# Linear attention and a highway layer on one core: one batch's query turned by DMA, weights in the output buffers, a new list of steps

## The chip, the core and the metric

The kernel runs on one core of a Trainium2 chip. The metric is the device time of one execution in microseconds (us). The engines work beside each other, each through its own list of instructions in order: PE (matrix products and transposes), DVE (vector operations), ACT (activations and copies, and some DMA issues), POOL (vector operations that do not touch PSUM), and SP, whose list holds DMA issues. An instruction waits at the head of its list until what it needs is there.

## The reference

With q, k and v of 8 batches, 8 heads, 576 positions and 64 columns each:

```
q_s = softmax of q over the 64 columns
k_s = softmax of k over the 576 positions
kv  = k_s^T v          # 64 x 64 for each batch and head
x   = q_s kv           # regrouped to 4608 tokens x 512
H   = max(x w_h, 0);  T = sigmoid(x w_t + b_t)
out = T * H + (1 - T) * x
```

Inputs and output are 32 bit floats; the kernel computes its products in 16 bit floats with sums in 32 bits.

## The kernel before

**Tiles.** A token p*9+j of a batch lies on partition p (64 of them) with j from 0 to 8, and two heads share the 128 partitions. A tile has 128 tokens: for each batch four tiles with two values of j, and for each pair of batches one tile with j = 8 of both. That makes 36 tiles; 0 to 3 belong to batch 0, 4 to 7 to batch 1, 8 to both, and so on; 27 to 30 belong to batch 6, 31 to 34 to batch 7, 35 (`LAST`) to both. `mate` names the neighbour with which a tile is stored.

**A batch.** `k`, `v`, `q` load it (three buffers of each). `ek` and `eq` are the exponentials on ACT, `vc` casts v. `kv` makes 72 small products (with a column of ones that gives the sum over positions), `kr` and `kn` divide by that sum and lay the result out in `kvb`. `qt` turns the exponentials of q in three groups (L280: eight, eight and two transposes of 128x128 on PE, into the PSUM tile qps), and `qc` (L291) copies each group out to the tile eq.

**A tile.** `xu` multiplies turned q by kv, with the sums of q beside; `rs` and `x` divide (DVE). `xt` turns x on PE, `xe` copies it out. `bw` seeds the PSUM bank of the gate with the bias: on ACT as a copy of a ready 128x512 tile, or on PE as one matmul. `mt` adds x w_t (four matmuls of 512 columns) and `mh` makes x w_h - x/2 with a weight that was halved and had half the identity subtracted (`whc`, `whd`). `th` is tanh of half the gate (ACT), `dd` the maximum of -x/2 and the product (DVE), `uu` is (tanh + 1) times d, and `oo` adds x (POOL). Where `uu` is marked `:P` the tile is "lifted": `ee` on POOL makes d + x, `uu` on POOL makes tanh times d, and `oo` adds these two; ACT's tanh then goes to SBUF. `st` stores.

**Order.** The order is written out by hand: `ORDER` (L16) is a list of steps, such as `xu_9_0` or `xe_9_0:D`, that the last loop (L433) works through; a suffix says which engine (A for ACT, D for DVE, P for POOL). Every engine gets its own instructions in this order. Nothing else places work; the tile framework adds the waits. `fill_n` is n matmuls on a blank tile, whose result nobody reads; they stand only ahead of the first large products. The loads are issued on SP, between the stores.

**Buffers.** Results of two mates share a 128x2x512 buffer of 32 bit floats (tag o32, three buffers); single tiles have 128x512 (tag o1). d, u, tanh and e of tiles have three buffers each (pool dp). PSUM has two banks for the gate (tps), two for the other product (gps), two for xu or kv, one for qps, one for the turned x.

**Steps that the prediction names.** `load_w` L191 and the weights' landing tiles L108; casts L199 to L211; `eq` L273; `qt` L280; `qc` L291; `xu` L299; `bw` L344; `mt` L354; `mh` L360; `th` L372; `ee` L385; `uu` L390; `oo` L403; `st` L414. The last tile's gate is worked in two halves of 256 columns, in one bank; its four stores of 64 rows and 256 columns go two on SP and two on ACT (L418).

Of the kernel before, what the change touches and what calls it, by code (L numbers as in the profile page):

```python
# [16 lines left out]
b_0 b_32 setuppool fill_16 setupdve k_0_0 v_0_0 v_0_2 k_0_2 q_0_0 w_h_0 q_0_4 bsplit w_h_2 fill_4 bp w_t_0 bc vc_0_0:A  # L17
w_t_2 bw_0:A ek_0_1 vc_0_2 k_1_0 ek_0_0 vc_0_3 vc_0_1:A ek_0_3 fill_30 kv_0_0 q_1_0 ek_0_2 kr_0_0 kn_0_0 fill_5 kv_0_1
eq_0_0 v_1_0 kr_0_1 kn_0_1 fill_6 qt_0_0 whc_0 k_1_2 qc_0_0 half fill_9 xu_1_0 xu_0_1 xu_0_0 eq_0_1 rs_0_1 rs_1_0
v_1_2 rs_0_0 x_1_0 bw_1:A x_0_0 fill_10 qt_0_1 x_0_1 whd_0 qc_0_1:A q_1_4 fill_2 xt_0_1 whc_2 xt_0_0 whd_1 whd_3  # L20
xe_0_1 fill_6 xu_2_0 whd_2 xe_0_0 xt_1_0 rs_2_0 mh_0_0 v_2_0 xe_1_0 x_2_0 mh_0_1 eq_0_2 wtc_0:D mh_1_0 wtc_2:D mt_0_0
dd_1 mt_0_1 dd_0 xu_3_0 th_0_0 xt_2_0 mt_1_0 rs_3_0 k_2_0 xe_2_0:D ek_1_0 uu_0_0 mh_2_0 th_1_0 x_3_0 eq_1_0 bw_2
uu_1_0 xt_3_0 mt_2_0 dd_2 ek_1_1 xe_3_0:D qt_1_0 oo_0_0 oo_1_0 q_2_0 th_2_0 vc_1_1:D mh_3_0 bw_3:A uu_2_0 ek_1_2
mt_3_0 qc_1_0 ek_1_3 dd_3 th_3_0 vc_1_0 oo_2_0 kv_1_0 vc_1_2 vc_1_3:A kr_1_0 st_1_0_0 uu_3_0 kv_1_1 kn_1_0 k_3_0 bw_4
kr_1_1 kn_1_1 eq_1_1 xu_5_0 eq_1_2 qt_1_1 rs_5_0 x_5_0 xu_4_0 bw_5 qc_1_1:A rs_4_0 st_1_0_1 xt_5_0 x_4_0 xu_4_1 v_3_0
qt_1_2 xu_6_0 vc_2_0:A qc_1_2:A q_3_0 xe_5_0:D rs_4_1 mh_5_0 x_4_1 rs_6_0 x_6_0 xt_4_0 mt_5_0 xe_4_0:D dd_5 xu_7_0
th_5_0 xt_4_1 mt_4_0 oo_3_0 rs_7_0 xe_4_1 mh_4_0 ek_2_2 xt_6_0 qt_0_2 mt_4_1 mh_4_1 ek_2_0 th_4_0 uu_5_0 xe_6_0:D
x_7_0 mh_6_0 dd_4 vc_2_2 oo_5_0 kv_2_0 uu_4_0 xt_7_0 kr_2_0 bw_6 bw_7:A qc_0_2:A eq_2_0 oo_4_0 dd_6 mt_6_0 kn_2_0
eq_2_1 qt_2_0 ee_6 st_5_0_1 xe_7_0:D xu_8_0 st_3_0_1 th_6_0 qc_2_0 mt_7_0 st_3_0_0 rs_8_0 uu_6_0:P bw_8:A k_4_0 x_8_0
qt_2_1 ek_3_2 xu_9_0 xt_8_0 mh_7_0 rs_9_0 x_9_0 xe_8_0 st_5_0_0 eq_2_2 xt_9_0 dd_7 ek_3_0 v_4_0 xu_10_0 mt_8_0 rs_10_0  # L30
oo_6_0 xe_9_0:D th_7_0 x_10_0 mh_8_0 th_8_0 uu_7_0 vc_3_0:A xt_10_0 mh_9_0 dd_8 xe_10_0:D vc_3_2 oo_7_0 q_4_0 bw_9:A
kv_3_0 uu_8_0 qc_2_1:A oo_8_0 bw_10 mh_10_0 kr_3_0 kn_3_0 eq_3_0 dd_9 xu_11_0 eq_3_1 mt_9_0 st_7_0_1 rs_11_0 ee_9
x_11_0 qt_3_0 st_7_0_0 th_9_0 dd_10 xt_11_0 xu_12_0 q_5_0 xe_11_0:D mt_10_0 uu_9_0:P rs_12_0 qc_3_0 mh_11_0 x_12_0
th_10_0 uu_10_0 xu_13_0 xt_12_0 ek_4_0 bw_11 rs_13_0 mt_11_0 xe_12_0:D x_13_0 k_5_0 eq_3_2 bw_12 dd_11 qt_2_2 th_11_0
xu_14_0 xt_13_0 ek_4_2 oo_9_0 oo_10_0 mt_12_0 rs_14_0 qc_2_2 uu_11_0 qt_3_1 x_14_0 xe_13_0 mh_12_0 bw_13:A qc_3_1
v_5_0 th_12_0 xt_14_0 xu_15_0 dd_12 xe_14_0 mh_13_0 rs_15_0 oo_11_0 vc_4_0:A uu_12_0 mh_14_0 x_15_0 bw_14 dd_14
st_10_0_0 eq_4_0 dd_13 st_10_0_1 vc_4_2 oo_12_0 kv_4_0 qt_3_2 mt_13_0 kr_4_0 qc_3_2 kn_4_0 k_6_0 xt_15_0 mt_14_0
th_13_0 xe_15_0 uu_13_0 xu_16_0 th_14_0 qt_4_0 rs_16_0 oo_13_0 mh_15_0 bw_15:A x_16_0 eq_4_1 uu_14_0 xu_17_0 qc_4_0
xt_16_0 oo_14_0 eq_5_0 bw_16 mt_15_0 xe_16_0:D rs_17_0 eq_5_2 x_17_0 mt_16_0 st_14_0_0 th_15_0 st_12_0_1 dd_15 xt_17_0
st_12_0_0 xu_18_0 th_16_0 uu_15_0:P xe_17_0:D mh_16_0 v_6_0 bw_17:A rs_18_0 x_18_0 ek_5_2 qt_4_1 ee_15 dd_16 xu_19_0  # L40
xt_18_0 ek_5_0 mh_17_0 rs_19_0 qc_4_1 xe_18_0:D qt_5_0 x_19_0 vc_5_0:A vc_5_2 q_6_0 mt_17_0 qc_5_0 xt_19_0 dd_17
kv_5_0 th_17_0 oo_15_0 uu_16_0 st_14_0_1 qt_5_2 mh_18_0 kr_5_0 bw_18:A xe_19_0:D kn_5_0 bw_19:A mt_18_0 dd_18 xu_20_0
mt_19_0 rs_20_0 x_20_0 qc_5_2:A eq_5_1 th_18_0 qt_5_1 ek_6_2 xu_21_0 xt_20_0 mh_19_0 xe_20_0 uu_18_0 rs_21_0 x_21_0
bw_20:A xt_21_0 dd_19 th_19_0 xu_22_0 mt_20_0 qc_5_1:A rs_22_0 oo_16_0 uu_17_0:P st_16_0_0 ee_17 oo_17_0 oo_18_0
uu_19_0 mh_20_0 x_22_0 xe_21_0 oo_19_0 th_20_0 xt_22_0 xu_23_0 dd_20 bw_21:A mh_21_0 vc_6_2 bw_22:A rs_23_0 x_23_0
eq_4_2 mt_21_0 uu_20_0:P ek_6_0 xe_22_0:D q_7_0 dd_21 qt_4_2 st_16_0_1 xu_24_0 mt_22_0 th_21_0 vc_6_0 k_7_0 rs_24_0
x_24_0 v_7_0 eq_6_0 mh_22_0 uu_21_0 ee_20 st_19_0_1 xt_23_0 th_22_0 qc_4_2 kv_6_0 st_19_0_0 xe_23_0:D bw_23:A oo_21_0
dd_22 eq_6_1 st_17_0_1 xt_24_0 qt_6_0 kr_6_0 kn_6_0 mh_23_0 xe_24_0 qc_6_0 eq_7_0 xu_25_0 mt_23_0 rs_25_0 x_25_0
bw_24:A qt_7_0 dd_23 eq_7_2 xu_26_0 th_23_0 xt_25_0 oo_20_0 uu_22_0:P st_21_0_0 ee_22 mh_24_0 rs_26_0 uu_23_0 oo_22_0
x_26_0 mt_24_0 xe_25_0:D dd_24 xu_27_0 xt_26_0 rs_27_0 oo_23_0 xe_26_0:D st_23_0_1 x_27_0 st_8_0_0 st_8_0_1 vc_7_2  # L50
st_21_0_1 qc_7_0:A bw_25:A ek_7_2 mt_25_0 th_24_0 qt_6_1 ek_7_0 uu_24_0 xt_27_0 xu_28_0 xe_27_0:D mh_25_0 th_25_0
rs_28_0 x_28_0 vc_7_0:A mh_26_0 dd_25 xt_28_0 bw_26:A kv_7_0 dd_26 eq_7_1 uu_25_0 mh_27_0 kr_7_0 qc_6_1:A kn_7_0
# [14 lines left out]
def kernel(  # L67
# [28 lines left out]
    op = pool("op", 3)  # L96
# [11 lines left out]
    w32 = {w: consts.tile([P, KC, DM], FP32, name="w32" + w) for w in "th"}  # L108
# [13 lines left out]
    def once(name, make):  # L122
        if name not in T:
            T[name] = make()
        return T[name]
# [15 lines left out]

    def columns(i, h):
        return slice(h * DM // 2, (h + 1) * DM // 2) if i == LAST else slice(0, DM)
# [47 lines left out]
    def load_w(e, w, c):  # L191
        src = dict(t=moe_w_t, h=moe_w_h)[w]
        nc.sync.dma_start(w32[w][:, c:c + 2], src.rearrange("(c p) n -> p c n", p=P)[:, c:c + 2])
# [5 lines left out]
    def wt_cast(e, c):  # L199
        if e == "D":  # L200
            nc.vector.tensor_scalar_mul(w16["t"][:, c:c + 2], w32["t"][:, c:c + 2], 1.0)
        else:
            nc.scalar.copy(w16["t"][:, c:c + 2], w32["t"][:, c:c + 2])

    def wh_cast(e, c):
        nc.vector.tensor_scalar_mul(w16["h"][:, c:c + 2], w32["h"][:, c:c + 2], 0.5)

    def wh_diag(e, c):
        cs = slice(c * P, (c + 1) * P)
        nc.vector.scalar_tensor_tensor(  # L210
            w16["h"][:, c, cs], w32["h"][:, c, cs], 0.5, half, op0=ALU.mult, op1=ALU.subtract)  # L211
# [60 lines left out]

    def eq(e, b, g):  # L273
        t = once(f"qe{b}", lambda: qep.tile([P, NJ, 4, D], FP16, tag="qe", name=f"qe_{b}"))
        j0, j1 = GROUPS[g]
        nc.scalar.activation(t[:, j0:j1].rearrange("p j c d -> p c j d"),  # L276
                             T[f"q32{b}"].rearrange("p c (j d) -> p c j d", j=NJ)[:, :, j0:j1], AF.Exp)
# [20 lines left out]

    def xu(e, i, k):  # L299
# [7 lines left out]
        for n in range(2 * k0, 2 * k1):  # L307
            kk, hh = n // 2, n % 2
            for w, b in enumerate(bs):
                rows = slice(0, P) if len(bs) == 1 else slice(64 * w, 64 * w + 64)  # L310
                dst = t[rows, kk - k0, 0:260].rearrange("p (s e) -> p s e", s=4)[:, hh:hh + 3:2]
                nc.tensor.matmul(dst, T[f"eq{b}_{jp // 2}"][:, jp % 2, n], kvb[b % NKV][:, hh, kk],  # L312
# [31 lines left out]
    def bw(e, i):  # L344
        t = T[f"tps{i}"] = ps_t.tile([P, DM], FP32, tag="tps", name=f"tps_{i}")
        if e == "A":
            nc.scalar.copy(t, ball)  # L347
        else:
            nc.tensor.matmul(t, ones, b16, start=True, stop=False, skip_group_check=True)
# [117 lines left out]
```

The softmax here doesn't subtract the row's maximum and nothing guards it: scores larger than these inputs give would overflow.

## Time and profile before

| what | value |
|---|---|
| three runs | 125.98, 126.94, 127.22 us |
| median | 126.94 us |
| span of the profiled execution, first to last instruction | 126.1 us |
| mean granted clock of PE | 0.977 |
| PE busy, instructions | 112.1 us, 1415 |
| DVE busy | 101.4 us, 237 |
| ACT busy | 92.8 us, 144 |
| POOL busy | 70.2 us, 71 |
| moved by DMA | 40.08 MB |
| matmul of 128x512, gate (L357) | 140 |
| transposes of q (L286) | 144 of 222 ns, eight in a row take 0.45 us |
| u on DVE, 128x512 (L396) | 27 of 687 ns |
| e, u on POOL (L388, L394) | 8 each, 1157 and 1155 ns |
| o on POOL (L412) | 27 of 1155 ns from u and x, 8 of 1154 ns from u and e |
| v cast of 128x1152 on POOL (L238) | 1143 ns |
| w_t cast of 128x1024 on DVE (L201) | 684 ns |
| copy of a turned group of q, 128x1024 (L295) | 677 ns on DVE, 1010 on ACT |

Times are us from the first instruction unless marked ns. A matmul's busy time is longer than the distance to the next, since matmuls are pipelined, so distances are taken from the starts in the timeline. "[1.19 <-DVE kvb L266]" at the end of a line of the timeline says how long the engine was idle ahead of it and what ended that. In the slices each digit is the busy share of a fortieth of the span in tenths. The rows of an engine ending in q (SPq, ACTq) are the issues of DMAs.

### The profile page before, as it was taken

The page shows a single profiled execution, that of the slowest core. Times are in us where ns is not written, and L with a number is a line of the kernel's source. Part 1 is how long each engine was busy: PE and PEld are TensorE (multiplying, and loading weights), DVE is VectorE, ACT ScalarE, POOL GpSimd, SP SyncE. Part 2 cuts the span into 40 slices and gives each one's busy share as a digit, 9 for nine tenths or more (in the row PEclk, how much of TensorE's full clock was granted, in tenths as well). Part 3 has the DMA queues.
Part 4 walks back from the last instruction along what each step waited for, and adds up shares of the span by engine and source line. Part 5 has one row for each costly group of instructions (what it writes and reads, how often), then busy time and mean ns, then how long its engine had stood idle before and what let it go on. Part 6 is the DMA issues. An engine that isn't in the chain of part 4 may idle for free.

```text
span 126.1 us, 3549 instructions
## 1 busy us (share of the span) xinstructions
PE 112.1 (89%) x1415; PEld 68.6 (54%) x1415; DVE 101.4 (80%) x237; ACT 92.8 (74%) x144; POOL 70.2 (56%) x71
## 2 busy tenths in 40 slices
PE   5798979994999799999999999999899999999800
PEld 4485854543755365556564666557456656555400
DVE  5504769996868779999989899989889989999640
ACT  4098363995747999968959979999899996557500
POOL 5030000485304694785716769999974896786610
PEclk9999999999599999999999999999999999999996
DMA  4999999999999999999999999999987363733994
GB/s 110 376 386 373 383 385 377 387 378 387 391 394 400 396 385 300 376 394 396 405 393 391 402 404 397 393 400 394 393 324 229 86 166 83 144 70 80 222 237 127
DMA packets 20372, 40.08 MB, mean 318 GB/s; under 512 B 1282, under 2 KB 3586, under 8 KB 20356
## 3 DMA queue, kind: packets, MB, share of 16 engines
q1 hardware_dynamic: 20192, 39.72, 90.1%
q8 instruction: 11, 0.18, 0.6%
q10 hardware_dynamic: 164, 0.14, 0.4%
q14 instruction: 5, 0.04, 0.1%
HBM read 30.41 MB, written 9.44 MB: 316 GB/s over the span
## 4 chain that ended last, share of the span: by engine, by line
PE 36%; DMA 22%; DVE 12%; POOL 9%; ACT 7%; SPq 5%; issue 3%; DVEq 0%; POOLq 0%; ACTq 0%
PE gps L363 11%; DMA q<-in_q_dram 9%; PE tps L357 9%; DMA w32h<-in_moe_w_h_dram 7%; POOL o L412 6%; DMA out_dram<-o 5%; PE xu L312 5%; PE qps L286 4%; DVE u L396 4%; PE turned L334 3%; DVE d L383 2%; ACT qe L276 2%; ACT ek L232 2%; PE kv L248 2%; PE turned L168 2%
## 5 line engine op out<-in xcount | busy, mean ns | idle before, releaser
L412 POOL TENSOR_TENSOR o<-u,x 128x512 f32<-128x512 f16 x27 | 31.2, 1155 | 33.2 <-DVE u L396 32.7
L363 PE MATMUL gps<-w16h,xT 128*128 128x512 f16 x144 | 36.9, 384 | 0.0
L357 PE MATMUL tps<-w16t,xT 128*128 128x512 f16 (+1 forms) x148 | 36.8, 373 | 0.0
L327 DVE TENSOR_TENSOR x<-xu,rs 128x512 f16<-128x512 f32 (+1 forms) x38 | 24.9, 659 | 1.2
L383 DVE SCALAR_TENSOR_TENSOR d<-x,gps 128x512 f16<-128x512 f16 x36 | 24.3, 679 | 1.0 <-PE gps L363 0.8
L379 ACT ACTIVATE tps<-tps 128x512 f32<-128x512 f32 (+1 forms) x29 | 16.4, 568 | 11.0 <-PE tps L357 9.6
L276 ACT ACTIVATE qe<-q 128x1024 f16<-128x1024 f32 (+1 forms) x24 | 19.8, 845 | 3.0 <-DMA q<-in_q_dram 3.0
L396 DVE SCALAR_TENSOR_TENSOR u<-tps,d 128x512 f16<-128x512 f32 (+1 forms) x29 | 19.3, 669 | 3.1 <-POOL o L412 1.4
L357 PEld LDWEIGHTS <-xT 128*128 128x128 f16 x148 | 13.6, 98 | 11.6
L363 PEld LDWEIGHTS <-xT 128*128 128x128 f16 x144 | 13.2, 99 | 11.9 <-issue 0.5
L232 ACT ACTIVATE ek<-k 128x1152 f16<-128x1152 f32 (+1 forms) x20 | 18.8, 966 | 0.2 <-DMA k<-in_k_dram 0.2
L347 ACT COPY tps<-ball 128x512 f32<-128x512 f32 x27 | 15.9, 594 | 3.4 <-DVE u L396 3.4
L238 POOL CAST v<-v 128x1152 f16<-128x1152 f32 (+1 forms) x11 | 10.6, 969 | 10.8 <-DMA v<-in_v_dram 9.6
L312 PE MATMUL xu<-kvb,eq 128*128 128x130 f16 (+1 forms) x160 | 15.0, 229 | 1.4 <-DVE kvb L266 1.2
L334 PE MATMUL turned<-idh,x 128*128 128x128 f16 x144 | 14.4, 222 | 0.2 <-ACT xT L341 0.2
L168 PE MATMUL turned<-blank 128*128 128x256 f16 x88 | 12.4, 295 | 2.2 <-POOL blank L147 1.3
L312 PEld LDWEIGHTS <-eq 128*128 128x128 f16 (+1 forms) x160 | 10.3, 103 | 6.1 <-DVE kvb L266 1.7
L286 PE MATMUL qps<-idh,qe 128*128 128x128 f16 x144 | 12.3, 222 | 1.3 <-ACT qe L276 1.2
L334 PEld LDWEIGHTS <-x 128*128 128x128 f16 x144 | 9.8, 99 | 6.0 <-DVE x L327 2.7
L286 PEld LDWEIGHTS <-qe 128*128 128x128 f16 x144 | 9.5, 99 | 5.5 <-ACT qe L276 2.5
L168 PEld LDWEIGHTS <-blank 128*128 128x128 f16 x88 | 9.0, 106 | 4.1 <-POOL blank L147 1.3
L394 POOL TENSOR_TENSOR u<-th,d 128x512 f16<-128x512 f16 x8 | 9.2, 1155 | 2.8 <-ACT th L377 1.3
(45 smaller groups left out, 111.4 us busy)
## 6 DMA issues: line engine op xcount, KB each, us to landing
out_dram<-o SPq DMA_DIRECT2D x28, 256.0 KB, 9.6
v<-in_v_dram SPq DMA_DIRECT2D x6, 1152.0 KB, 13.5
k<-in_k_dram SPq DMA_DIRECT2D x6, 1152.0 KB, 13.9
q<-in_q_dram SPq DMA_DIRECT2D x6, 1152.0 KB, 14.0
k<-in_k_dram SPq DMA_DIRECT2D x4, 576.0 KB, 9.4
v<-in_v_dram SPq DMA_DIRECT2D x4, 576.0 KB, 6.6
out_dram<-o SPq DMA_DIRECT2D x14, 128.0 KB, 3.0
q<-in_q_dram SPq DMA_DIRECT2D x2, 640.0 KB, 11.4
```

Source lines behind the costliest of these rows:

```text
L168: nc.tensor.matmul(spare, blank[:, 0:P], blank[:, 0:2 * P], start=True, stop=True, skip_group_check=True)
L232: nc.scalar.activation(t[:, :, c:c + n].rearrange("p j c d -> p c j d"), T[f"k32{b}"][:, c:c + n].rearrange("p c (j d) -> p c j d", j=NJ), ...
L276: nc.scalar.activation(t[:, j0:j1].rearrange("p j c d -> p c j d"), T[f"q32{b}"].rearrange("p c (j d) -> p c j d", j=NJ)[:, :, j0:j1], AF.Exp)
L286: nc.tensor.matmul(t[:, (j - j0) // 2, 2 * kk:2 * kk + 2, (j - j0) % 2], T[f"qe{b}"][:, j, 2 * kk:2 * kk + 2].rearrange("p c d -> p (c d)" ...
L312: nc.tensor.matmul(dst, T[f"eq{b}_{jp // 2}"][:, jp % 2, n], kvb[b % NKV][:, hh, kk], start=True, stop=True, skip_group_check=True)
L327: nc.vector.tensor_mul(t[:, k0:k1], sums(i, k)[:, :, :, 0:64], T[f"rs{i}_{k}"][:, 0:k1 - k0].unsqueeze(3).to_broadcast([P, k1 - k0, 4, D]))
L334: nc.tensor.matmul(t[:, n], T[f"x{i}"][:, n * P:(n + 1) * P], idh, is_transpose=True, start=True, stop=True, skip_group_check=True)
L357: nc.tensor.matmul(T[f"tps{i}"][:, cs], T[f"xT{i}"][:, n], w16["t"][:, n, cs], start=False, stop=(n == 3), skip_group_check=True)
L363: nc.tensor.matmul(t, T[f"xT{i}"][:, n], w16["h"][:, n], start=(n == 0), stop=(n == 3), skip_group_check=True)
L383: nc.vector.scalar_tensor_tensor(t, T[f"x{i}"], -0.5, T[f"gps{i}"], op0=ALU.mult, op1=ALU.max)
L396: nc.vector.scalar_tensor_tensor(t[:, cs], T[f"tps{i}"][:, cs], 1.0, T[f"d{i}"][:, cs], op0=ALU.add, op1=ALU.mult)
L412: eng.tensor_add(t[:, cs], T[f"u{i}"][:, cs], T[f"{'e' if lifted(i) else 'x'}{i}"][:, cs])
```

## The change

It has six parts.

1. **Batch 7's query is turned by DMA.** Steps `dt_7_0` and `dt_7_1` each issue one transposing DMA on SP from the exponentials (64 partitions of 18 x 128 halves of 16 bits each) into a new tile eqd. `eq` writes batch 7 in another layout, two activations of 128x1152 in place of three; `qt_7` and `qc_7` are gone, and `xu` takes its weights from eqd.
2. **Weights land in output buffers.** The pool of o32 has seven buffers in place of three; the four loads of 128x2x512 weights take four of them first, and the separate tiles of weights in 32 bits are gone. w_t can be cast on POOL, and is.
3. **The last tile.** Each half of its gate has its own PSUM bank (the second takes that of qps), seeded on its own; its o halves go to POOL and DVE; its halves are stored with one DMA each, both batches in one (tile 8, 17 and 26 too).
4. **Stores on either queue.** A store marked `:A` is issued by ACT: nine are, in place of two.
5. **Halved tiles.** Tiles 0 and 4 may take their halves in either order.
6. **A new list of steps.** Lifted tiles are 0, 1, 2, 3, 4, 7, 8, 10, 11, 12, 14, 16, 18, 20, 21, 25, 27, 28 (18 in place of 8); bias seeds on PE are those of 0, 1, 2, 3, 4, 5, 7 and half of 35 (in place of 2, 4, 5, 6, 10, 11, 12, 14, 16); fills are 122 in place of 88.

The diff, cut:

```
-b_0 b_32 setuppool fill_16 setupdve k_0_0 v_0_0 v_0_2 k_0_2 q_0_0 w_h_0 q_0_4 bsplit w_h_2 fill_4 bp w_t_0 bc vc_0_0:A
-w_t_2 bw_0:A ek_0_1 vc_0_2 k_1_0 ek_0_0 vc_0_3 vc_0_1:A ek_0_3 fill_30 kv_0_0 q_1_0 ek_0_2 kr_0_0 kn_0_0 fill_5 kv_0_1
-eq_0_0 v_1_0 kr_0_1 kn_0_1 fill_6 qt_0_0 whc_0 k_1_2 qc_0_0 half fill_9 xu_1_0 xu_0_1 xu_0_0 eq_0_1 rs_0_1 rs_1_0
...
+b_0 b_32 q_0_0 v_0_0 eq_0_0 setupdve k_0_0 bsplit k_0_2 v_0_2 setuppool ek_0_0 vc_0_0 fill_30 vc_0_3 fill_30 q_0_4 half
+qt_0_0 w_h_0 ek_0_3 vc_0_1:D w_h_2 bp fill_30 w_t_0 ek_0_2 qc_0_0:A vc_0_2:D bc ek_0_1 w_t_2 fill_12 kv_0_0 eq_0_1
+kr_0_0 kv_0_1 kn_0_0 bw_0 qt_0_1 bw_3 kr_0_1 kn_0_1 xu_0_0 k_1_0 v_1_0 xu_1_0 whc_0 qc_0_1:A xu_0_1 wtc_0:P wtc_2:P
+rs_1_0 rs_0_1 whc_2 rs_0_0 eq_0_2 vc_1_1 x_0_0 x_1_0 whd_2 fill_20 x_0_1 xu_3_0 v_1_2 xt_0_0 xt_0_1 k_1_2 xe_0_0 xe_0_1
+q_1_0 q_1_4 whd_0 rs_3_0 xt_1_0 mt_0_0 mt_0_1 whd_3 xe_1_0 x_3_0 whd_1 mh_0_1 ek_1_0 mh_1_0 xu_2_0 xt_3_0 qt_0_2 mh_0_0
...
+oo_19_0 ee_21 rs_26_0 th_23_0 xe_25_0:D st_7_0_0 uu_21_0:P bw_24:A mh_23_0 eq_7_1 x_26_0 mh_24_0 xt_26_0 dd_23 xu_27_0
+eq_7_0 v_7_0 uu_23_0 oo_21_0 bw_25:A rs_27_0 oo_22_0 mt_24_0 xe_26_0:D eq_6_2 st_10_0_1 x_27_0 mh_25_0 dd_24 xu_29_0
+dt_7_0 ek_7_2 st_8_0_0 dt_7_1 mt_25_0 xt_27_0 dd_25 rs_29_0 th_24_0 vc_7_2:A oo_23_0 mh_26_0 vc_7_0 x_29_0 xe_27_0:D
...
+th_35_1 st_33_0_1 uu_34_0 dd_35 uu_35_1 th_35_0 st_33_0_0:A uu_35_0 oo_34_0 st_34_0_0 oo_35_0 st_34_0_1:A oo_35_1:D
+st_35_1_0 st_35_0_0:A
...
-    op = pool("op", 3)
+    op = pool("op", 7)
...
-    w32 = {w: consts.tile([P, KC, DM], FP32, name="w32" + w) for w in "th"}
...
-        nc.sync.dma_start(w32[w][:, c:c + 2], src.rearrange("(c p) n -> p c n", p=P)[:, c:c + 2])
+        T[f"w{w}{c}"] = op.tile([P, 2, DM], FP32, tag="o32", name=f"w32{w}_{c}")
+        nc.sync.dma_start(T[f"w{w}{c}"], src.rearrange("(c p) n -> p c n", p=P)[:, c:c + 2])
...
+        if b in BY_DMA:
+            t = once(f"qe{b}", lambda: qep.tile([P, 2 * NJ, 2 * D], FP16, tag="qe", name=f"qe_{b}"))
+            nc.scalar.activation(
+                t[:, g * NJ:g * NJ + NJ].rearrange("p j (w d) -> p w j d", w=2),
+                T[f"q32{b}"][:, 2 * g:2 * g + 2].rearrange("p w (j d) -> p w j d", j=NJ), AF.Exp)
+            return
...
+    def dt(e, b, hh):
+        t = once(f"eqd{b}", lambda: eqp.tile([P, 2, 2 * NJ, NP], FP16, tag="eqd", bufs=2, name=f"eqd_{b}"))
+        eng = nc.scalar if e == "A" else nc.sync
+        eng.dma_start(t[:, hh], T[f"qe{b}"][NP * hh:NP * hh + NP], transpose=True)
+
+    def turned_q(b, jp, n):
+        if b not in BY_DMA:
+            return T[f"eq{b}_{jp // 2}"][:, jp % 2, n]
+        j = (n // 2) * NJ + 2 * jp
+        return T[f"eqd{b}"][:, n % 2, j:j + (2 if jp < 4 else 1)].rearrange("p s t -> p (s t)")
...
+    def bw(e, i, h=0):
+        bank = (ps_t, "tps") if i < LAST or h == 0 else (ps_q, "qps")
+        t = T[gate(i, h)] = bank[0].tile([P, DM], FP32, tag=bank[1], name=f"tps_{i}_{h}")
...
-        eng = nc.vector if e == "D" or i == LAST else nc.gpsimd
+        eng = nc.vector if e == "D" else nc.gpsimd
...
-        eng = nc.scalar if i == LAST and r else nc.sync
+        eng = nc.scalar if e == "A" else nc.sync
...
-            eng.dma_start(dst[:, 8], T[f"o{i}"][rows, cs])
+            ends = out[b * S:(b + 2) * S, cs].rearrange("(r j) n -> r j n", j=NJ)
+            eng.dma_start(ends[:, 8], T[f"o{i}"][:, cs])
```

SP's own order of loads and stores around the change: before, it is q_5, k_5, v_5, two stores of tile pair 10, k_6, three stores (14, 12, 12), v_6, q_6, two stores, q_7, one store, k_7, v_7. After, it is v_5, k_5, one store of pair 1, q_5, v_6, one store of pair 10, k_6, one store, q_6, three stores (7, 3, 5), q_7, k_7, one store, v_7, one store, dt_7_0, the store of 8, dt_7_1, and the rest of the stores; ACT issues two stores of pairs 3 and 1 shortly ahead of the seed of tile 16.

## The prediction

> **What bounds the kernel now.** I read the page's slices first, then the windows of 5 us, then the timeline around the weak windows and the end. The slices (each 3.15 us):
>
> ```profile
> PE   5798979994999799999999999999899999999800
> POOL 5030000485304694785716769999974896786610
> PEclk9999999999599999999999999999999999999996
> DMA  4999999999999999999999999999987363733994
> ```
>
> DMA is full until about 91 us, PE from about 45 us to its last matmul, POOL is half empty. DMA is not the end: the last batch's loads land at 89.6 (q, the chain of waits) and about 96 (v, awaited by POOL), and PE has work until 119.2. The weak windows (columns: window, its length, busy us of PE, PEld, DVE, ACT, POOL, granted clock, DMA share, GB/s):
>
> ```profile
> 20.00:25.00 5.00, 5.00 (x34) 2.51 (x33) 4.80 (x10) 3.16 (x7) 1.23 (x2) 1.00 1.07 389
> 25.00:30.00 5.00, 4.03 (x92) 2.29 (x90) 4.54 (x10) 4.93 (x9) 4.22 (x5) 1.00 1.05 378
> 30.00:35.00 5.00, 4.01 (x31) 2.84 (x32) 4.03 (x13) 2.55 (x4) 1.53 (x2) 0.66 1.05 389
> 40.00:45.00 5.00, 4.17 (x80) 2.58 (x69) 3.98 (x9) 4.30 (x7) 3.18 (x3) 1.00 1.05 396
> 105.00:110.00 5.00, 5.00 (x38) 2.85 (x37) 4.71 (x10) 2.81 (x6) 3.04 (x3) 1.00 0.61 127
> ```
>
> PE loses 1.0, 1.0 and 0.8 us in three of them, and from 30 to 35 the clock drops to 0.66. The timeline names the places:
>
> ```profile
> 19.30 1.89 PE L363 MATMUL gps<-w16h,xT 128*128 128x512 f16 x8
> ...
> 30.99 0.41 PE L312 MATMUL xu<-kvb,eq 128*128 128x130 f16 x4 [1.19 <-DVE kvb L266]
> ...
> 33.73 1.64 PE L363 MATMUL gps<-w16h,xT 128*128 128x512 f16 x4
> ...
> 42.57 0.62 PE L286 MATMUL qps<-idh,qe 128*128 128x128 f16 x8 [0.83 <-ACT qe L276]
> ...
> 118.18 1.04 PE L357 MATMUL tps<-w16t,xT 128*128 128x256 f16 x8
> ...
> 120.93 0.76 DVE L412 TENSOR_TENSOR o<-u,x 128x256 f32<-128x256 f16 x2
> 121.39 1.18 ACTq L425 DMA_DIRECT2D out_dram<-o  x2
> 122.36 1.20 SPq L425 DMA_DIRECT2D out_dram<-o  x2
> ```
>
> The large products start at 19.3; batch 1's first xu waits for its kv chain; four large matmuls at 33.7 take 1.64 instead of 1.03 (about 0.6 lost); PE ends at 119.2 and the span 6.9 us later, through tanh, u, o and four small stores. So the bound is PE's in-order list, with a slow opening and a serial tail.
>
> [...]
>
> **The change, part by part.** Large matmuls follow each other every 0.216 us in the timeline (four in 0.865), so a tile costs PE 1.73, plus xu 0.235 and its own transposes 0.22.
>
> *Batch 7's query off PE.* 18 of 144 transposes go. Eight take 0.45 in the chain of waits, so 18 x 0.056 = 1.0 us off PE. The three evictions (two of 128x1024, one of 128x256) go too; eq_7 becomes two activations of 128x1152 (1.16 by the ek row) for 1.06 + 1.06 + 0.42.
>
> *Fewer bias matmuls.* 9 become 7 and a half: 1.5 x 0.215 = 0.3 off PE; ACT gets one more seed of 0.594 and a half one (0.37, by the 128x256 tanh).
>
> *Who does what.* Lifted tiles (u and e on POOL) go from 8 to 18. DVE: 10 u x 0.687 = -6.9, two casts of w_t -1.3, the other moves nearly cancel (about +0.3): 101.4 to 93.5. POOL: 10 x (1.155 + 1.157) = +23.1, two v casts fewer -2.3, two w_t casts +2.0 (1.143 x 1024/1152 each), half an o +0.6: 70.2 to 93.6. ACT stays near 93, but issues 9 stores instead of 2 (0.54 each: +3.8 us of its queue). Two of them (tiles 3 and 1) stand before the seeds and tanh of tiles 14 to 16; their o are long done, so I charge the issue alone, hidden since ACT has 8 to 30% idle in the windows from 50 us on, save some full ones; without that cover tanh, then u, is late by the same 0.54 each.
>
> *Opening.* Bytes to each load at 379 GB/s with the observed landing of w_h_0 (3.4 MB, 12.8) give w_t_2 at about 18.6 in both. The new list puts 90 fills ahead of kv_0_0 plus 12: 20 cold at about 0.175, then 0.112 each, 3.5 + 9.2; with qt_0_0 and bp in between (0.9) and a start at 1.3, kv_0_0 comes at 14.9 (9.67 before). Then kr/kn to 17.05, the first xu, 20 fills to 19.75, x_0_1 at 20.8 behind whc and whd on DVE, xe, xt_1_0, and mt_0_0 at 21.7: 2.4 later than before's first product. I keep this loss. Against it: v_1_2 and k_1_2 are loaded ahead of q_1_0, kv_1_0 is fed earlier, and bw, xt_2 and the products of tile 2 stand where PE stood idle. Walking the PE list by these durations, with ek_1_3 at 28.7 and eq_1_0 at 29.8 on ACT, I get mh_5 ended at 35.9 with xu_6 and qt_0_2 already done, where before has the rest at 36.2: 0.3 + 0.24 + 0.11 = 0.65 ahead. Then kv_2 at 41.4, after more work than in before, and xu_9 behind mh_7, so that kn_2's latency is covered: tiles 0 to 7 and xu_9 are done at 44.6 and qt_2_2 too, against 46.14: 1.5 ahead.
>
> *Loads and stores.* 9 stores of 0.26 MB stand before v_7 instead of 16: 7 x 0.26 / 0.39 = 4.7 us earlier. Seven output buffers allow that (the weights' 16 KB a partition are reused). I cost it at nothing: PE from 45 to 119 has only some 2.2 us of idle, which this does not remove. If stores came first, q_7 would again be just in time (wait of 0.4 at qps).
>
> *Middle and end of PE.* From 44.6, 28 tiles x 1.73 = 48.4, 26 xu and the pairs 6.7, xt 5.95, four batches of qt 4.05, five kv 3.6, a half bias: 68.8; with the same 2.2 idle PE ends at 115.6. Before's own sum from 46.14 is 70.9 + 2.2 = 119.2. So PE ends 3.6 us earlier: 1.5 from the opening, 2.1 here (1.0 transposes, 0.1 the qt_2_2 already done, 1.0 for the five bias matmuls that before still has in this stretch).
>
> *Transposing DMAs.* eq_7_1 and eq_7_0 follow th_23: by the list after it mt_23 ends at 87.7, so eq_7_0 at about 91.2, when the loads (v_7 about 91) are in. The first use, xu_31, has 14 half products (12.1) and 2.3 of xu and xt after it: 115.6 - 14.4 = 101.2. Both together have 10 us. Each moves 64 x 1152 x 2 bytes = 147 KB. [...] The new wait is SP's, for eq_7_0: behind it stand st_8, st_14 and every later store of SP, and behind those POOL's o, when the seven buffers are full. In a 10 us hold POOL makes four o, two pairs, so this cover is thin if the stores have fallen behind; then o waits, u's buffers fill, and DVE is next.
>
> *Last tile.* Halves in their own banks, one store each, on SP and ACT, o halves on POOL and DVE at once. After PE's end: tanh 0.37, u 0.42, o on POOL 0.58 (half of 1.155), hops of 0.1, an issue of 0.6, landing 2.2, end 0.5: 5.2 instead of 6.9, -1.7.
>
> **Sum.** 126.1 - 3.6 - 1.7 = 120.8. POOL now has 62 us of work in the 70 us from 44 on and three buffers of d, and ACT issues stores amid its work: I add 0.8 for such waits, 121.6, 4.5 less. The profiled span of 126.1 is within the runs (125.98 to 127.22); from their median of 126.94 I forecast 122.4.
>
> **Rivals.** *A, POOL becomes the bound.* For: tiles 0, 1, 3, 2, 4 and 8, 10, 11, 12 are lifted, 3.47 us of POOL each against PE's 2.4 a tile; d has three buffers, so dd waits and DVE's whole queue behind it (rs, x, xT), then PE. Against: by my walk d of 10 comes free at 57.6 and is wanted at 58.5. Each microsecond of POOL lag beyond that is a microsecond of PE; with 4 of it, 126.4.
>
> *B, slower: late transposing DMAs.* [...] It decides from a landing of 105.7 (a tie) or 107 (slower by 1%). [...]
>
> *C, [...]* 2.4 late: 124.8.
>
> *D, the list does nothing* since only the 1.3 us of PE and the tail count: 126.94 - 3.0 = 123.9, if the late start (2.4) eats the opening's gain. I count this in the main case's range.
>
> **Numbers.** Main case (with D) 0.62, 120.3 to 124.3 by itself; C 0.10; A 0.13; B 0.15. A change of 1% is about what a measurement here can tell. Faster: 0.62 + 0.10 = 0.72; same: most of A, 0.12; slower: B and the rest of A, 0.16. The range to 8 in 10 goes from 120.3 to 128.0.
>
> **What would show it.** First large matmul at 21 to 22; no wait over 0.5 us at batch 1's xu and no slice of low clock near 35; 126 transposes of q on PE; PE's last matmul near 116; POOL busy 93, DVE 93; both transposes landed before xu_31; 5.2 us from PE's end to the span's. Wrong if dd waits for POOL, if xu_31 waits for a DMA, or if the opening is over 2 us later by tile 8.

## The result, and the profile after

The changed kernel takes 131.75 us (median of four runs, 130.86 to 132.73) against 126.47 us for the kernel before, run beside it: a ratio of 1.041, with a 95% interval from 1.035 to 1.047. It is slower by 4%; the forecast was 122.4. The ratios here and below leave out executions over 1.5% above the fastest of the same kernel: one of four in runs 3 and 5, two of twenty in run 8, and twelve of twenty in run 2, whose ratio over all twenty would be 1.016 in place of 1.0038. The profiled execution of the changed kernel has a span of 129.6 us, against the 120.8 that the sum gave before its allowance of 0.8 for waits.

Engine totals came out as forecast: DVE 94.6 us busy (forecast 93.5), ACT 92.7 (93), POOL 92.3 (93.6). So the question is not how much work there is, but what it waits for. The slices of the page after (each 3.24 us):

```profile
PE   5999976798999999999989999999999999996000
DMA  3999999999999999999999999991048999999894
GB/s 65 382 395 371 384 390 390 365 380 391 393 382 392 392 391 388 389 392 396 397 385 400 402 398 401 392 380 65 0 79 193 218 272 226 267 273 205 222 216 128
```

Read the DMA row and the row of rates together. Before, DMA is full to about 91 us and then has room to spare until the end. After, it is full to 87, nearly empty for three slices (65, 0 and 79 GB/s), and then busy again up to the last slice, but at only 193 to 273 GB/s. PE's row has no hole; it merely stops three slices ahead of the end. The windows of 5 us say the same with PE beside it (window, length, busy us of PE, PEld, DVE, ACT, POOL, granted clock, DMA share, GB/s):

```profile
80.00:85.00 5.00, 5.00 (x113) 3.15 (x111) 4.51 (x11) 5.00 (x8) 4.77 (x5) 1.00 1.05 393
...
90.00:95.00 5.00, 5.00 (x42) 2.69 (x41) 4.76 (x11) 4.80 (x8) 4.92 (x5) 1.00 0.00 0
...
120.00:125.00 5.00, 0.00 (x0) 0.00 (x0) 0.75 (x1) 0.00 (x0) 1.95 (x2) 0.75 0.92 214
```

From 90 to 95 nothing at all is moved while every engine is busy. From 120 to 125 PE is done and DMA works at 0.92 of its time: what is left is stores. SP's own timeline shows why nothing was moved:

```profile
77.03 2.24 SPq L454 DMA_DIRECT2D out_dram<-o  x1
94.08 1.42 SPq L316 DMA_TRANSPOSE eqd<-qe  x1
...
97.03 1.32 SPq L316 DMA_TRANSPOSE eqd<-qe  x1
98.45 12.18 SPq L454 DMA_DIRECT2D out_dram<-o  x10
```

Between 79.3 and 94.1 SP issues nothing. The list of waits names what it waits for, and what POOL's last outputs wait for at the other end:

```profile
SPq L316 <- ACT qe L290: 15.6, 1, 15.6
...
SPq L454 <- POOL o L445: 8.0, 4, 7.1
...
POOL o L445 <- DMA out_dram<-o: 5.1, 1, 5.1
```

SP stood 15.6 us at the first transposing DMA, for batch 7's exponentials, which come late in ACT's order. By then ten stores of 0.262 MB had been issued, 2.6 of 9.44 MB; the other 6.8 MB had to go out after 94, with no load beside them. From 97 to 125 they move at a mean of 231 GB/s, at a DMA share of 0.94. The 7.1 us of the second line lie at 56 to 63 us, amid the loads; after 96 SP's longest wait for an o is 1.7 us. At the very end POOL can't write o of tile 34 and the last tile's first half, nor DVE its second half, because none of the three buffers for single tiles has come free: the stores that would free one are still on their way.

Three more things from the timeline after, for the forecast's steps (PE's first large product and start of kv_2, the first use of DMA-turned q, PE's last products, the last tile's o and store):

```profile
24.12 1.03 PE L386 MATMUL tps<-w16t,xT 128*128 128x512 f16 x4
...
44.05 0.78 PE L254 MATMUL kv<-v,ek 64*64 64x65 f16 x72
...
103.81 0.40 PE L337 MATMUL xu<-kvb,eqd 128*128 128x130 f16 x4
...
117.79 1.04 PE L386 MATMUL tps<-w16t,xT 128*128 128x256 f16 x8
122.76 1.95 POOL L445 TENSOR_TENSOR o<-u,x 128x512 f32<-128x512 f16 x2 [5.07 <-DMA out_dram<-o]
123.43 0.75 DVE L445 TENSOR_TENSOR o<-u,x 128x256 f32<-128x256 f16 x1 [3.58 <-DMA out_dram<-o]
124.94 1.02 SPq L459 DMA_DIRECT2D out_dram<-o  x1
```

PE ends at 118.83 where 115.6 was forecast (3.2 late), and the span ends 10.8 us after that where 5.2 was forecast (5.6 late). Together 8.8, the whole miss in the span. The use of eqd at 103.81 has no bracket: it waited for nothing.

### The profile page after: what moved, and what is told of

It reads as the page before. It is cut to its first block, busy times and chain, and to the rows that moved or that the text cites. A ratio compares the mean times of both kernels' runs of the same rounds, so it can differ in the third digit from the quotient of the medians.

```text
span 129.6 us, 3577 instructions
## 1 busy us (share of the span) xinstructions
PE 113.6 (88%) x1430; PEld 70.6 (54%) x1430; DVE 94.6 (73%) x226; ACT 92.7 (71%) x142; POOL 92.3 (71%) x92
## 3 DMA queue, kind: packets, MB, share of 16 engines
HBM read 30.41 MB, written 9.44 MB: 307 GB/s over the span
## 4 chain that ended last, share of the span: by engine, by line
PE 50%; DVE 20%; ACT 15%; issue 4%; DMA 2%; SPq 2%; POOL 1%; POOLq 1%; ACTq 0%; DVEq 0%
PE gps L394 13%; PE tps L386 13%; PE turned L172 11%; DVE x L352 5%; PE xu L337 4%; PE turned L359 4%; DVE d L414 4%; ACT ek L238 3%; DVE u L429 3%; ACT v L244 3%; PE qps L300 2%; DMA out_dram<-o 2%; ACT xT L366 2%; PE kv L254 2%; ACT tps L374 2%
## 5 line engine op out<-in xcount | busy, mean ns | idle before, releaser
L445 POOL TENSOR_TENSOR o<-u,x 128x512 f32<-128x512 f16 (+1 forms) x18 | 20.3, 1138 | 7.5 <-DMA out_dram<-o 5.1
L427 POOL TENSOR_TENSOR u<-th,d 128x512 f16<-128x512 f16 x18 | 20.7, 1155 | 5.4 <-DVE rs L346 5.2
L445 POOL TENSOR_TENSOR o<-u,e 128x512 f32<-128x512 f16 x18 | 20.7, 1155 | 1.6 <-DVE xT L366 1.0
L420 POOL TENSOR_TENSOR e<-d,x 128x512 f16<-128x512 f16 x18 | 20.7, 1154 | 0.5 <-DVE d L414 0.5
L290 ACT ACTIVATE qe<-q 128x1024 f16<-128x1024 f32 (+1 forms) x21 | 17.0, 841 | 2.0 <-DMA q<-in_q_dram 2.0
L374 ACT COPY tps<-ball 128x512 f32<-128x512 f32 (+1 forms) x29 | 16.8, 585 | 1.4 <-DVE u L429 1.2
L172 PE MATMUL turned<-blank 128*128 128x256 f16 x122 | 16.3, 301 | 1.3 <-POOL blank L151 1.3
L410 ACT ACTIVATE tps<-tps 128x512 f32<-128x512 f32 (+1 forms) x19 | 10.8, 566 | 7.2 <-PE tps L386 7.0
L172 PEld LDWEIGHTS <-blank 128*128 128x128 f16 x122 | 13.1, 108 | 4.1 <-POOL blank L151 1.3
L429 DVE SCALAR_TENSOR_TENSOR u<-tps,d 128x512 f16<-128x512 f32 (+1 forms) x19 | 12.4, 659 | 2.0 <-ACT tps L410 1.0
## 6 DMA issues: line engine op xcount, KB each, us to landing
k<-in_k_dram SPq DMA_DIRECT2D x6, 1152.0 KB, 15.1
```

Source lines behind the costliest of these rows:

```text
L172: nc.tensor.matmul(spare, blank[:, 0:P], blank[:, 0:2 * P], start=True, stop=True, skip_group_check=True)
L374: nc.scalar.copy(t[:, cs], ball[:, cs])
L420: eng.tensor_add(T[f"e{i}"], T[f"d{i}"], T[f"x{i}"])
L427: eng.tensor_mul(t, T[f"th{i}"], T[f"d{i}"])
L445: eng.tensor_add(t[:, cs], T[f"u{i}"][:, cs], T[f"{'e' if lifted(i) else 'x'}{i}"][:, cs])
```

## The experiments

**Theory.** SP's list is in order, so its wait for eq_7_0 holds up stores whose data were long ready. Held stores lose their place beside the loads and run alone at the end, where they are slower, and the end then waits for them. **Rivals:** the transposing DMAs themselves disturb the transfers; POOL's extra work makes the outputs late; or the late first product alone is enough. Each run gives a ratio to the kernel before with its 95% interval, and the span of its profile; "the tail" is the time from PE's end to the span's end. Line numbers in some kernels are one higher, since their list of steps has one line more.

**1. The transposing DMAs on ACT's queue.**

```
-dt_7_0 ... dt_7_1
+dt_7_0:A ... dt_7_1:A
```

> Both transposing DMAs are issued by ACT, so SP no longer waits for eq_7_0 from 79.3 to 94.1 us. Store theory (the end is set by stores that were held back and then run alone at about 215 to 270 GB/s): SP is free for st_8, st_14 and st_21, 0.79 MB, and then waits at 95.4 for the o of tile 23, which stands next in its list; 0.79 MB at 245 GB/s is 3.2 us, so the span falls from 129.6 to about 126.5, with PE's end unchanged near 118.8. PE theory (the late opening, 24.1 us to the first large product, makes the loss): no change, 129.6. Theory that the transposing DMAs themselves slow the stores: no change or worse, since they then run beside stores.

Measured: 1.0447 [1.036, 1.0533], span 130.5. A miss. SP got past its place, but only to the store of tile 23, whose o is ready at about 92, and stood there; later it stood for o of tile 28 until 114.7. PE ended at 121.7, 2.9 later than in the changed kernel, with two transposing issues of 1.4 and 3.05 us amid ACT's work; the tail fell from 10.8 to 8.8. This run does not clear SP's list, it moves the head of the queue to the next late item.

**2. Eight ready stores ahead of the transposing DMAs.** Still on SP, the DMAs where they were. One of the eight, of tile 17, was on ACT's queue and goes to SP with the others.

```
+st_8_0_0 st_14_0_0 st_12_0_0 st_12_0_1 st_14_0_1 st_16_0_0 st_16_0_1 st_17_0_0
 dt_7_0 ... dt_7_1
-(the same eight further down the list)
```

> Eight stores whose o is long done (tiles 8, 12, 14, 16, 17; about 1.97 MB) are moved ahead of the first transposing DMA in SP's list, nothing else. Store theory: these are written while the last loads are still read, so after 94 us 6.8 - 2.0 = 4.8 MB remain, 19.6 us at 245 GB/s from 95, or 115: the stores stop being the bound and the span is PE's end (118.8) plus 5 to 6, about 124.5. PE theory: 129.6. Slow-transpose theory: some gain, but the rate of the stores after 98 us stays low.

Measured: 1.0038 [0.9995, 1.008], span 124.9, as expected. SP's timeline in this run:

```profile
81.00 9.43 SPq L454 DMA_DIRECT2D out_dram<-o  x6
...
92.93 3.71 SPq L316 DMA_TRANSPOSE eqd<-qe  x2
```

The moved stores go out one behind another between 79 and 91.8, beside the last loads (392 and 398 GB/s in the windows 80 to 90). Of the 4.7 us of span that this saves, 3.6 are in the tail (7.2 us from PE's end, 10.8 before the edit) and 1.2 in PE's end, by which the first large product is earlier in this execution too (22.96), for a reason that comes below. By the runs' ratios the edit takes off 3.7% of the time before, 4.7 us (2.5% over all its executions), and it is a change of order in the list of stores and nothing else. SP now comes early to the store of tile 28 and waits 5.3 us for its o, until 110.65; this is the "second hold" of the next runs. In the changed kernel, where SP reaches that store only at 112.8, its waits for these stores are 0.5 us at most.

**3. Batch 7's query turned on PE again, all else as changed.** eq_7 in three activations, qt_7 and qc_7 back in the list, no transposing DMA.

```
-dt_7_0 dt_7_1
+eq_7_2   qt_7_0 qc_7_0   qt_7_1 qc_7_1:A   qt_7_2 qc_7_2
```

> Batch 7's query is turned by PE as in the kernel before (18 more PE transposes, three copies), the transposing DMAs are gone; all else is as in the changed kernel. Store theory: SP is then held only by the o of tile 23 until about 95, as in the run with the transposing DMAs on ACT; span 126 to 127. Slow-transpose theory: clearly better than that run, near 124. PE theory: 130.6, since PE has 1.0 us more.

Measured: 1.0364 [1.0275, 1.0452], span 128.9. A miss: taking the transposing DMAs out gains only 0.7 of span, and the ratio's interval overlaps that of the changed kernel. PE ends 1.4 later (120.2) and the tail is 8.7. SP again went on to the store of tile 23 and waited 10.1 us there, with ready stores behind it:

```profile
81.09 20.16 SPq L455 DMA_DIRECT2D out_dram<-o  x10
```

**4. As 3, with the store of tile 23 in the place of the transposing DMAs.** So SP is held again, by an ordinary store.

```
-st_8_0_0 ... st_23_0_1
+oo_23_0 st_23_0_1 st_8_0_0
```

> As the run with PE turning the query, but the store of tile 23, whose o is ready at about 95 us, stands where the first transposing DMA stood, and the store of tile 8 behind it: SP is held as long as in the changed kernel, with no transposing DMA at all. Store theory: as slow as the changed kernel, 129.5 to 131. Slow-transpose theory: about 126, no slower than the run without the hold.

Measured: 1.0434 [1.0324, 1.0544], span 129.5, as slow as the changed kernel, without a single transposing DMA:

```profile
77.14 17.77 SPq L455 DMA_DIRECT2D out_dram<-o  x2
```

Two stores in 17.8 us: the second is the held one, with a wait of 14.6. The rival that the transposing DMAs disturb the transfers falls: without any the kernel is as slow. That this longer hold costs more than the 10.1 us of run 3 is not shown, since the two intervals overlap.

**5. The second hold eased alone.** POOL makes o of tile 28 ahead of 29, four stores are placed by when their data are ready.

```
-oo_29_0 ee_28 oo_28_0
+ee_28 oo_28_0 oo_29_0
-st_28_0_0 st_30_0_0 st_25_0_1:A st_16_0_1 (late)
+st_28_0_0 and st_30_0_0 beside their mates, st_25_0_1:A beside st_25_0_0:A, st_16_0_1 ahead of st_26_0_0
```

> Only the second hold of SP is eased in the changed kernel (the o of tile 28 is made ahead of that of 29 on POOL; both stores of 28 and of 30 follow each other, those of 16 and 25 stand ahead of them); the wait of SP for eq_7_0 stays. Theory of two holds in a row, either of which is enough: the stores held until 94 us keep DMA full from 95 on anyway (6.8 MB at about 240 GB/s is 28 us), so span 129 to 130, no gain. Rival (only the second hold sets the end, since removing the first alone in two runs gave nothing): about 125.

Measured: 1.0327 [1.0245, 1.0409], span 128.7. Its interval overlaps that of the changed kernel. The wait for qe is still 15.4 us. While the first hold stands, SP comes to the stores of tile 28 too late to wait for them, so there is hardly a second hold to ease.

**6. Edits 2 and 5 together:** the first hold taken away, the second eased.

> The eight ready stores ahead of the transposing DMAs and the second hold eased. Theory of two holds: PE's end plus about 6, since 0.5 to 1 MB less is left after 110; span 123.5 to 124.5, 0.5 to 1.5 below the run with the first alone. Rival (the end is PE's end and the last tile's own path): no change, 124.9.

Measured: 1.0013 [0.9986, 1.004], span 123.4. The interval overlaps that of run 2, so a gain from the second edit is not shown here either. The profile is of the fastest of twenty executions (125.45 us; the median is 126.65). The DMA rows of its page, SP's stores near the second hold, and the end:

```profile
DMA  3999999999999999999999999999997889939875
GB/s 65 388 396 372 384 388 393 373 372 390 396 379 390 393 393 387 391 391 388 399 396 392 406 398 399 403 393 399 395 341 171 138 182 203 232 82 226 268 174 152
```

```profile
104.68 0.35 SPq L459 DMA_DIRECT2D out_dram<-o  x1
109.39 4.34 SPq L454 DMA_DIRECT2D out_dram<-o  x4
...
117.12 1.04 PE L386 MATMUL tps<-w16t,xT 128*128 128x256 f16 x8
...
119.33 0.72 POOL L445 TENSOR_TENSOR o<-u,x 128x256 f32<-128x256 f16 x1 [0.35 <-DVE u L429]
119.57 0.54 SPq L459 DMA_DIRECT2D out_dram<-o  x1
```

The hole from 90 to 95 is gone, the full rate lasts to 90 because stores share it, and no o waits for a buffer. SP still waits 4.3 us for o of tile 28, until 109.4, so the second hold is shorter by 1.0 and not gone. From PE's end at 118.16 to the span's end are 5.2 us, as forecast for the last tile; the median execution is 1.2 us longer, and where is not shown. The forecast's other miss is still there: PE's end at 118.2 instead of 115.6.

**7. Edit 6 and shorter fills in the opening.**

```
-fill_30 fill_30 fill_30 fill_12 kv_0_0 ... fill_20
+fill_30 fill_30 fill_16 kv_0_0 ... fill_14
```

> As the run with both holds eased, with 60 of fills ahead of qt_0_0 kept, but 16 for 42 ahead of kv_0_0 and 14 for 20 behind the first xu. PE theory of the rest of the loss (the fills put kv_0_0 at 15 to 16 where its operands are there at 13.1): first large product 2 to 2.5 us earlier, PE's end and the span 2 earlier, 121 to 122. Rival (the data of batches 1 and 2 or POOL set the pace after the opening): the first product is earlier, PE's end is not, 123.5 to 124.5.

Measured: 123.99 us against 126.18, 0.9807 [0.9748, 0.9866], span 121.7. It is faster than both kernels, than the one before by 1.3 to 2.5%. PE:

```profile
20.29 1.03 PE L386 MATMUL tps<-w16t,xT 128*128 128x512 f16 x4
...
114.67 1.04 PE L386 MATMUL tps<-w16t,xT 128*128 128x256 f16 x8
```

The first large product is 2.5 us earlier than in run 6 and PE's end 2.45 earlier (115.71): what is saved in the opening reaches PE's end in full. By the medians run 7 is 2.7 us faster than run 6; the spans of the two profiles differ by only 1.7, since that of run 6 is of its fastest execution, and since here the tail is 6.0 and POOL waits 1.5 us for a buffer near the end.

**8. The kernel before's list of steps under the changed code.** Only what the code needs: a second seed for the last tile, one store per pair for 8, 17, 26 and 35. No DMA-turned query, before's engines and order.

> The list of the kernel before under the new code: seven output buffers that the weights share, the last tile's halves in their own banks and stored with one DMA each, batch 7 turned by PE; lifted tiles, fills, loads and nearly all stores stand as before. Theory (the new list costs, the code does not): as the kernel before or up to 1.5 us faster by the shorter tail. Rival (the shared buffers or the last tile's code cost time): slower than before.

Measured: 0.9964 [0.9929, 0.9998], span 123.8. Seven buffers, weights landing in them, the last tile's own banks and paired stores do no harm. What costs is in the new list; by run 3 it is not the transposing DMAs themselves.

**9. Transfers alone, spread.** The loads of batches 0 to 3, then those of 4 to 7 with two stores behind each, then the remaining stores; nothing is computed and the stores write zeros.

```
 for b in 0..7:  for w in k, v, q:
     load(w, b)
+    if b >= 4: store(2)
+store(the rest)
```

> Only transfers, all on SP, of this kernel's shapes: the loads of four batches alone (14.2 MB), then those of four more with two stores behind each load (14.2 MB and about 6.2 MB), then the other stores alone; zeros are stored, nothing is computed. Store theory (stores alone move at 215 to 270 GB/s, stores beside reads cost no more than their bytes at the full rate): about 390, 390 and 240 GB/s in the three stretches. Rival (the low rate after 95 us comes from the compute engines or from the waits on o, not from the stores): about 390 in all three.

Measured: 104.79 us, span 103.0 (one execution). Loads alone run at 391 to 393 GB/s, loads and stores together at 400 to 403, and the window 95 to 100, with stores alone, at 219. Most stores of that tail, however, are of half the size (128 KB), hence run 12.

**10. The w_t casts moved from POOL to ACT, on top of 7.**

```
-wtc_0:P wtc_2:P
+wtc_0 (ahead of eq_0_2)   wtc_2 (behind xe_0_1)
```

> As the run with both holds eased and short fills, with the two casts of w_t moved from POOL to ACT, one ahead of eq_0_2 and one behind tile 0's xe. Theory that POOL's cast slows DVE's beside it (1.05 and 1.25 us in the changed kernel for 0.69 before): both casts of w_h back at 0.69, first large product 0.7 to 0.9 us earlier, span 120.5 to 121.2. Rival (DVE's casts were slow for another reason): they stay at 1.05 to 1.25 and nothing is gained.

Measured: 0.9818 [0.9735, 0.9901], span 122.7. A miss, no gain over run 7. The casts of w_h on DVE, which the move was to free, take 0.69 and 0.66 us here, and took 0.69 and 0.66 in run 7 too: with the shorter fills both start ahead of POOL's first cast there (15.77 and 16.65, against 17.16), so there was nothing left to win. The first large product is at 20.39 (20.29 in run 7).

**11. The shorter fills alone, both holds left in.**

> The changed kernel with the short fills alone; SP's holds stay. Two-cause theory: the first large product 2.5 earlier (21.5), and since all later steps move with it, eq_7_0 and so the end of SP's wait too (94.1 to 91.6): the span falls by about 2.5 to 127, and the distance from PE's end to the span's stays near 10. Rival (the stores alone set the end, whatever PE does): 129.6 stays.

Measured: 1.011 [1.0026, 1.0194], span 125.8, 3.8 less than the changed kernel, where 2.5 was expected.

```profile
20.34 1.03 PE L386 MATMUL tps<-w16t,xT 128*128 128x512 f16 x4
...
114.01 1.04 PE L386 MATMUL tps<-w16t,xT 128*128 128x256 f16 x8
```

```profile
SPq L316 <- ACT qe L290: 11.8, 1, 11.8
```

The first large product comes at 20.34, 3.8 earlier, PE ends at 115.05, 3.8 earlier, and SP's first hold ends at 90.3, again 3.8 earlier, with a wait of 11.8 in place of 15.6. The tail stays at 10.8. So the late opening was not just PE's loss: SP's hold ended later by as much, since eq_7_0 stands behind th_23 in ACT's list and th_23 waits for PE.

**12. Transfers alone, stores last.** As run 9, without the stores between the loads.

```
-    if b >= 4: store(2)
```

> The transfers of the run before, with the order alone changed: all 24 loads of k, v and q first, then all 44 stores, back to back, every one ready from the start; nothing is computed and the stores write zeros. Theory (stores that run with no load beside them are slow in themselves): the loads take 28.31 MB at 391 GB/s, to about 75 us; the 9.44 MB of stores then run at 220 to 270 GB/s, 35 to 43 us, and the span is 110 to 118 us against 103.0 with the stores spread. Rival (the low rates in the changed kernel come from stores that were not ready or from SP's issuing): the stores run at about 390 GB/s here, 24 us, and the span is 99 to 103 us, as with the stores spread.

Measured: 111.93 us, span 110.2 (one execution); 7.2 us longer than run 9 for the same bytes. In the windows DMA share and GB/s are the last two columns (only DVE and POOL have instructions here):

```profile
70.00:75.00 5.00, 0.00 (x0) 0.00 (x0) 1.00 1.05 392
...
90.00:95.00 5.00, 0.00 (x0) 0.00 (x0) 1.00 0.85 259
95.00:100.00 5.00, 0.00 (x0) 0.00 (x0) 1.00 0.87 254
```

Every store is ready, most are of 256 KB, and from 85 to 100 they still run at 254 to 259 GB/s, at a mean share of 0.84 to 0.87 of the DMA engines. So the low rate at the end of the changed kernel is no sign of late producers: these stores are slow with nothing beside them. The rival, 390 GB/s here and a span of about 100, falls as far as it blames the producers. Its other half, SP's issuing, is not tested, since SP issues every store here too; nor does this run tell a store from its shape, for which see the last section.

## Why the prediction was wrong

The four kernels that differ in the two suspected causes make a square (PE's end, tail and span of the profile in us; ratio of the runs):

| | long fills | short fills |
|---|---|---|
| SP held | 118.83 + 10.8 = 129.6; 1.041 (changed kernel) | 115.05 + 10.8 = 125.8; 1.011 (run 11) |
| first hold removed, second eased | 118.16 + 5.2 = 123.4; 1.001 (run 6) | 115.71 + 6.0 = 121.7; 0.981 (run 7) |

Down a column the tail changes by 4.8 to 5.6 and the ratio by 3.0 to 4.0%; along a row PE's end changes by 2.5 to 3.8 and the ratio by 2.1 to 3.0%. The two causes are nearly independent. That the lower right corner is close to the forecast of 121.6 is luck: it has 32 fills fewer than the kernel that was forecast.

**The step that failed: "Loads and stores", "I cost it at nothing".** The step looked at the good side, loads that end 4.7 us earlier (they end 7.5 earlier: v_7 lands at 88.5, where before it was at 96.0), and asked only whether PE would gain from it. It did not ask where the stores go that were taken out of the loads' stretch. Under "Transposing DMAs" SP's new wait was seen and the queue behind it named, but the cover was called thin only for the case that buffers run out. The price is another: while SP waits, the DMA engines run out of work (none from 90 to 95), and 6.8 MB remain for a stretch where they take 6.8 MB / 0.25 MB per us = 27 us by run 12's rate, instead of 17 at the 0.4 MB per us of run 9's mixed stretch. From 95 that leads to 122, and at the measured mean of 231 GB/s to 124, before the last tile's own stores have gone. The tail's 5.6 us too many are this. Runs 2 and 6 show it by removing the hold, where the tail falls to 7.2 and 5.2; run 4 is as slow as the changed kernel with a hold of 14.6 us and without the DMAs. It is the first hold that counts: 124.9 without it alone, 128.7 with the second alone eased, and for the second no gain is shown.

The row that should have warned was on the page before: from 95 us on, its DMA row lies between 3 and 9 tenths at 70 to 237 GB/s, so even half-idle engines moved little, and 105 to 110 shows a share of 0.61 for 127 GB/s. I read "DMA is not the end" from it; it also said that a byte stored after the loads costs more DMA time than one moved during them: 0.61 for 127 GB/s is 1.8 times as much a byte as 1.05 for 389.

**"Opening", first product at 21.7, was mis-sized.** It came at 24.12, and kv_2 at 44.05 in place of 41.4: 2.6 late by tile 8, which the prediction had named as a sign of being wrong. One part is the execution: the first 60 fills took 9.19 us here, against 8.16 to 8.42 in five other profiles with the same fills (runs 1 to 4 and 6) and 9.37 in run 5; the step's rates make that 3.5 + 40 x 0.112 = 7.98. In those five kv_0_0 is at 14.9 to 15.1, as forecast, but the first product still comes at 22.8 to 23.0, 1.1 to 1.3 later than forecast: the stretch from kv_0_0 to it takes 7.9 us, not 6.8. A part of that is a DVE cast of w_h that meets a POOL cast of w_t (0.57 us in run 6, two such casts and 0.9 in the changed kernel's profile); the rest I have not divided. That the long fills delay PE whatever the execution is shown by runs 7 and 11; this loss the forecast saw (2.4 later than before) and kept.

**"Middle and end of PE" was right.** From kv_2 to PE's end took 74.8 us; the forecast has 115.6 - 41.4 = 74.2. In run 6 the same stretch is 75.5. The sum for transposes, bias matmuls and 18 lifted tiles comes out as a whole; its parts were not measured one by one.

**"Transposing DMAs": they were cheap, the wait was the cost.** Each took 1.3 to 1.4 us of SP's queue and 4.0 us from issue to landing; in run 2, with stores ahead of them, 1.6 to 2.0 and 4.2 to 4.7, and in runs 7 and 10 the two issues together took 4.1 and 5.1. They were issued 2.9 us later than the 91.2 forecast, and xu_31 still waited for nothing. Rivals B (late transposes) and C (2.4 us late) fall by that line; B had the right sign for the wrong reason. The price that I took for one was an assumption: the kernel before has no such DMA. All these have one size, so how the price grows with the size is not shown.

**"Last tile", 5.2 us, was right** in run 6's profile, where its o finds a free buffer; in the changed kernel the tail is 10.8.

**Rival A, POOL as the bound,** falls in its strong form: the longest waits of DVE's and PE's lists for POOL in the changed kernel are 0.3 us (u for o) and, at the start, the blank tile. POOL sets the time in one place, o of tile 28, and only once the first hold is gone: SP waits 5.3 us for it in run 2. **Rival D** is half right: with the opening as long as it was, run 6 gives no gain over before (1.0013), and the tail and transposes only paid for the late start.

## What to carry to other kernels

Before moving a wait to the head of a queue that also issues stores, list every transfer behind it and ask when its data were ready; put ready ones ahead of the wait. In these runs a store was cheapest beside loads (400 to 403 GB/s together in run 9, 245 to 259 for stores alone in run 12), and worth moving there even when no buffer was short: total bytes say little, the question is how many of them are left when the loads end. And here the fills taken out ahead of the first products came back in full at PE's end (2.45 us in run 7, 3.8 in run 11), since they stood in front of work whose operands were there.

## What the runs showed of the hardware

**Stores of 64 partitions were slow when they ran alone.** 391 to 393 GB/s for loads and 400 to 403 mixed (run 9), 245 to 259 for stores alone in run 12 (85 to 105 us), and 219 in the tail of run 9. That the direction makes the difference is not shown: every store of these two runs reads 64 of the 128 partitions, and every load fills all 128. The trace of the changed kernel points to the shape. From 116.1 to 118 us only stores of partitions 64 to 127 are under way (tiles 28, 30, 25, 16 and 31), at 212 GB/s and a share of 1.00. From 102 to 107 stores of both halves are, with no load beside them: 267 GB/s in the mean at a share of 0.92, 307 from 104 to 105 and from 106 to 107. So stores alone can move more than 212; but run 12, where the halves alternate, stays at 245 to 259, and why, with the engines' share near 0.85, is open. A kernel whose late stores cover 128 partitions was not run.

**A DVE cast took longer beside a POOL cast:** 1.05 and 1.25 us in the changed kernel, where the same two take 0.69 and 0.66 in run 7, begun ahead of POOL's first, and again in run 10, where POOL casts no weights; in run 6 the first, begun ahead of POOL's, takes 0.69 and the second, beside it, 1.26. The changed kernel's timeline:

```profile
18.12 1.04 POOL L209 CAST w16t<-w32t 128x1024 f16<-128x1024 f32 x1 [6.39 <-DMA w32t<-in_moe_w_t_dram]
18.66 1.05 DVE L212 TENSOR_SCALAR w16h<-w32h 128x1024 f16<-128x1024 f32 x1
...
19.48 1.13 POOL L209 CAST w16t<-w32t 128x1024 f16<-128x1024 f32 x1 [0.31 <-DMA w32t<-in_moe_w_t_dram]
19.89 1.25 DVE L212 TENSOR_SCALAR w16h<-w32h 128x1024 f16<-128x1024 f32 x1
```

POOL's casts end at 19.16 and 20.61, DVE's at 19.71 and 21.14: 0.55 and 0.53 after them. Of the 0.66 to 0.69 that the cast takes alone, all but some 0.13 us would fit in after POOL's end. The times agree with a cast that stood still meanwhile, but how is not shown.

**The first 60 fills took a different time in each execution,** 8.16 to 9.37 us in the seven profiles with this opening (the changed kernel and runs 1 to 6), while the 42 fills behind them took 4.75 in every one. In the changed kernel PE does 11 fills from 2 to 4 us and 20 from 8 to 10, with a granted clock of 1.00 shown in both windows; what slows the early ones is not shown. The first large product of the seven comes at 22.75 to 24.17, so a forecast of one execution of this opening can be off by the 1.4 us between them.
